# Normalized-query/key attention on one core: moving the Q and K transposes from TensorE to the DMA engines

## The chip, the cores and the metric

One core of one Trainium2 chip. The metric is device microseconds (us) of one execution. Executions of one kernel agree within about 0.3%. Engines in the profile: PE = TensorE matmuls, PEld = TensorE weight loads, DVE = VectorE, ACT = ScalarE, POOL = GpSimd, SP = SyncE (SPq is its queue of issued DMAs).

## The reference

```python
# q, k, v: (1, 32, 2048, 20) bf16; t: (32,) bf16
qn = q / (jnp.sqrt((q * q).sum(axis=-1, keepdims=True)) + eps)
kn = k / (jnp.sqrt((k * k).sum(axis=-1, keepdims=True)) + eps)
logits = jnp.einsum('bhqd,bhkd->bhqk', qn, kn) * t[None, :, None, None]
attn = softmax(logits)
return jnp.einsum('bhqk,bhkd->bhqd', attn, v)
```

There are 32 heads of 2048 rows, and a row has only 20 elements.

## The kernel before

Work is laid out as 32 heads x 2 passes (halves of the queries) x 16 rounds, 1024 rounds in all. In a round TensorE makes a 128 x 1024 block of scores S in PSUM (two matmuls), ScalarE takes its exponential into SBUF, and two rounds later TensorE multiplies it by V and accumulates (two PV matmuls). There are two S buffers.

```python
def plan_exp(self, n):
    Sps = self.Sps[n % 2]                 # 2 score buffers in PSUM
    Pb = self.Pbuf[n % self.NB]
    ... e.activation(Pb[:], Sps[:], AF.Exp), [(E, self.eS[n])] ...
def plan_S(self, n, h, p, kg, qq):
    ...                                   # cut
    if n >= 2:
        waits.append((A, self.a_exp[n - 2]))   # buffer is free again
```

Each head's q and k arrive with rows on partitions. VectorE normalizes them, TensorE transposes them in batches of 8 small matmuls (128 x 20 each) into PSUM, and VectorE copies the batch to SBUF. A head has four such batches, put at rounds 9 and 13 of the two passes of the head before. The output is transposed back in the same way, in two batches of 4 at rounds 2 and 6 of each pass.

```python
def plan_qt_transposes(self, h, bb):      # kt: the same with kn
    for i in range(n):                    # n = 8
        out_ap = self.TQK[0:self.D, P * i:P * (i + 1)]
        in_ap = qnb[:, tt, :]
        fn = lambda e, o=out_ap, a=in_ap: e.transpose(o, a, self.ident_bf[:, :])
        ...                               # cut
def plan_qt_copies(self, h, bb):
    dst = QTb[0:self.D, self.QH * bb:self.QH * (bb + 1)]
    ... e.tensor_copy(out=dst, in_=self.TQK[0:self.D, :]) ...
# in the loop over rounds
            if bg_idx < len(bgtasks):     # squared sums of heads 4 to 31 on VectorE
                self.ss_task(hh, qk)      # one task a round until done
```

Of the kernel before, what the change touches and what calls it, by code (L numbers as in the profile page):

```python
# [9 lines left out]
P = 128  # L10
# [19 lines left out]
class _Builder:  # L30
# [90 lines left out]
    def alloc(self):  # L121
# [7 lines left out]
        self.sDO = [self.sem("sDO0"), self.sem("sDO1")]  # L129
        groups = []  # L130
        hs = 0
        for he in (self.HA, min(self.H, 12), self.H):
            if he > hs:
                groups.append((hs, he))
                hs = he
# [22 lines left out]
        self.qn = [self.sb("qn%d" % b, [P, T, D], bf) for b in range(2)]  # L158
        self.kn = [self.sb("kn%d" % b, [P, T, D], bf) for b in range(2)]
# [8 lines left out]
        self.TQK = self.ps("TQK", [32, QH], bf)  # L168
# [3 lines left out]
    def plan(self):  # L172
# [11 lines left out]
        for gi, (hs, he) in enumerate(self.groups):  # L184
            for tens, store, sems in ((q, self.q_all, self.dq), (k, self.k_all, self.dk), (v, self.v_all, self.dv)):
                src = tens[0, hs:he].rearrange("h (p t) d -> p h (t d)", p=P)
                dst = store[:, hs:he, :, :].rearrange("p h t d -> p h (t d)")
                sy(lambda e, d=dst, s=src: e.dma_start(d, s), (), sems[gi], 16)

# [5 lines left out]
        self.g_qt = {}  # L195
        self.g_kt = {}
        for b in range(2):
            vb, qtb, ktb = self.vaug[b], self.QT[b], self.KT[b]
            self.g_qt[b] = gp(lambda e, qtb=qtb: e.memset(qtb[:], 0.0))  # L199
            self.g_kt[b] = gp(lambda e, ktb=ktb: e.memset(ktb[:], 0.0))  # L200
            gp(lambda e, vb=vb: e.memset(vb[:], 0.0))  # L201
            self.g_vaug[b] = gp(lambda e, vb=vb: e.memset(vb[:, :, D:D + 1], 1.0))
# [24 lines left out]
        self.v_qtcp_done = {}  # L227
        self.v_ktcp_done = {}
        self.tr_qt = {}
        self.tr_kt = {}  # L230
# [4 lines left out]
        self.last_tqkread_v = 0  # L235
# [6 lines left out]
        self.plan_qt_transposes(0, 0)  # L242
        self.plan_qt_copies(0, 0)
        self.plan_kt_transposes(0, 0)
        self.plan_kt_copies(0, 0)
# [12 lines left out]
        for n in range(NT):  # L258
# [13 lines left out]
            if h == 0 and p == 0:  # L272
                if r == 0:
                    self.plan_kt_transposes(0, 1)
                elif r == 3:
                    self.plan_qt_transposes(0, 1)
            if p == 0:
                if h >= 1:
                    if r == 2:
                        self.plan_O_transposes(h - 1, 1, 0)  # L280
                        self.plan_O_transposes(h - 1, 1, 1)
                    elif r == 6:
                        self.plan_O_transposes(h - 1, 1, 2)
                        self.plan_O_transposes(h - 1, 1, 3)
                if h + 1 < H:
                    if r == 9:
                        self.plan_qt_transposes(h + 1, 0)
                    elif r == 13:
                        self.plan_qt_transposes(h + 1, 1)
            else:  # L290
                if r == 2:
                    self.plan_O_transposes(h, 0, 0)
                    self.plan_O_transposes(h, 0, 1)
                elif r == 6:
                    self.plan_O_transposes(h, 0, 2)
                    self.plan_O_transposes(h, 0, 3)
                if h + 1 < H:
                    if r == 9:
                        self.plan_kt_transposes(h + 1, 0)
                    elif r == 13:  # L300
                        self.plan_kt_transposes(h + 1, 1)
            if h == 0 and p == 0:
                if r == 1:
                    self.plan_kt_copies(0, 1)
                elif r == 4:
                    self.plan_qt_copies(0, 1)
            if p == 0:
                if r == 0 and h >= 1:
                    self.plan_copyout(h - 1, 1, 0)
                if r == 1 and h >= 1:  # L310
                    self.plan_copyout(h - 1, 1, 1)
                if r == 2 and h + 1 < H:
                    self.plan_prep(h + 1)
                if r == 7 and h >= 1:
                    self.plan_divides(h - 1, 1)
                if h + 1 < H:
                    if r == 10:
                        self.plan_qt_copies(h + 1, 0)
                    elif r == 14:
                        self.plan_qt_copies(h + 1, 1)  # L320
            else:
                if r == 0:
                    self.plan_copyout(h, 0, 0)
                elif r == 1:
                    self.plan_copyout(h, 0, 1)
                elif r == 7:
                    self.plan_divides(h, 0)
                if h + 1 < H:
                    if r == 10:
                        self.plan_kt_copies(h + 1, 0)  # L330
                    elif r == 14:
                        self.plan_kt_copies(h + 1, 1)
            if bg_idx < len(bgtasks):
# [67 lines left out]
    def plan_prep(self, h):  # L401
# [3 lines left out]
        vaug, qnb, knb = self.vaug[b], self.qn[b], self.kn[b]  # L405
# [11 lines left out]
        w = [(self.dq[gi], 16)]  # L417
        if h >= 2:
            w.append((TR, self.tr_qt[(h - 2, 1)]))
        v2 = self.op("vector", lambda e: e.tensor_tensor(out=qnb[:], in0=qsrc,  # L420
# [6 lines left out]
        if h >= 2:  # L427
            w.append((TR, self.tr_kt[(h - 2, 1)]))
        v3 = self.op("vector", lambda e: e.tensor_tensor(out=knb[:], in0=ksrc,  # L429
# [3 lines left out]

    def plan_qt_transposes(self, h, bb):
        V, TR, G = self.sV, self.sTR, self.sG
        b = h % 2
        qnb = self.qn[b]
        n = self.QH // P
        waits0 = [(V, max(self.v_qn[h], self.last_tqkread_v)), (G, self.g_ident)]
        val = None  # L440
        for i in range(n):
            tt = bb * n + i
            out_ap = self.TQK[0:self.D, P * i:P * (i + 1)]
            in_ap = qnb[:, tt, :]
            fn = lambda e, o=out_ap, a=in_ap: e.transpose(o, a, self.ident_bf[:, :])  # L445
            val = self.op("tensor", fn, waits0 if i == 0 else (),
                          inc=(TR if i == n - 1 else None), chain=False)
        self.tr_qt[(h, bb)] = val
        return val

    def plan_kt_transposes(self, h, bb):
        V, TR, G = self.sV, self.sTR, self.sG
        b = h % 2
        knb = self.kn[b]
        n = self.QH // P
        waits0 = [(V, max(self.v_kn[h], self.last_tqkread_v)), (G, self.g_ident)]
        val = None
        for i in range(n):
            tt = bb * n + i
            out_ap = self.TQK[0:self.D, P * i:P * (i + 1)]  # L460
            in_ap = knb[:, tt, :]
            fn = lambda e, o=out_ap, a=in_ap: e.transpose(o, a, self.ident_bf[:, :])  # L462
            val = self.op("tensor", fn, waits0 if i == 0 else (),
                          inc=(TR if i == n - 1 else None), chain=False)
        self.tr_kt[(h, bb)] = val
        return val

    def plan_qt_copies(self, h, bb):
        V, TR, E, G = self.sV, self.sTR, self.sE, self.sG
        b = h % 2  # L470
        QTb = self.QT[b]
        waits = [(TR, self.tr_qt[(h, bb)])]
        if h >= 2:
            waits.append((E, self.ePV[self.end_round_of_head(h - 2)]))
        val = None
        waits.append((G, self.g_qt[b]))
        dst = QTb[0:self.D, self.QH * bb:self.QH * (bb + 1)]
        src = self.TQK[0:self.D, :]
        val = self.op("vector", lambda e: e.tensor_copy(out=dst, in_=src), waits, inc=V)  # L479
        self.last_tqkread_v = val  # L480
        self.v_qtcp_done[(h, bb)] = val
        return val

    def plan_kt_copies(self, h, bb):
        V, TR, E, G = self.sV, self.sTR, self.sE, self.sG
        b = h % 2
        KTb = self.KT[b]
        waits = [(TR, self.tr_kt[(h, bb)]), (G, self.g_kt[b])]
        if h >= 2:
            waits.append((E, self.ePV[self.end_round_of_head(h - 2)]))  # L490
        src = self.TQK[0:self.D, :]
        dst = KTb[0:self.D, self.QH * bb:self.QH * (bb + 1)]
        val = self.op("vector", lambda e: e.tensor_copy(out=dst, in_=src), waits, inc=V)  # L493
        self.last_tqkread_v = val
        self.v_ktcp_done[(h, bb)] = val
        return val

    def plan_S(self, n, h, p, kg, qq):
# [4 lines left out]
        kb = 0 if kg < self.KG // 2 else 1  # L503
        qb = min(p, 1)
        waits = [(V, max(self.v_ktcp_done[(h, kb)], self.v_qtcp_done[(h, qb)]))]
# [150 lines left out]
```

## Time and profile before

| | before |
|---|---|
| median of the runs, us | 1077.85 (1077.7 to 1078.46) |
| ScalarE busy, us | 973.5 (90%) |
| TensorE matmul busy, us | 1047.9 (97%) |
| VectorE busy, us | 308.1 (29%) |
| time of one pass in the steady stretch, us | 16.22 |

The page's groups of instructions of the kernel before. A line is: source line, engine, operation, out<-in, shapes, count | busy us, mean ns of one | idle us just before them and what ended it.

```profile
L550 ACT ACTIVATE Pbf<-Sps 128x1024 bf16<-128x1024 f32 x1024 | 966.0, 1031 | 89.7 <-PE Sps L516 89.7
L516 PE MATMUL Sps<-QT,KT 128*128 128x512 bf16 x2048 | 618.6, 384 | 5.2 <-ACT Pbf L550 4.4
...
L479 DVE COPY QT<-TQK 20x1024 bf16<-20x1024 bf16 x64 | 43.4, 679 | 179.4 <-PE TQK L445 178.9
```

The exponentials are busy for 966 us, and ScalarE stands idle for 90 us more, waiting for S.

Two lines of the chain of waits of the kernel before, shares of the span by engine and by line:

```profile
PE 91%; DVE 5%; ACT 1%; POOL 1%; issue 0%; ACTq 0%; DVEq 0%; POOLq 0%
PE Sps L516 42%; PE OACC L541 39%; PE TOps L589 4%; PE TQK L462 3%; PE TQK L445 3%; DVE ss_all L370 2%; DVE sq_tmp L367 1%; ACT Pbf L550 1%; DVE O_sb L569 0%; DVE QT L479 0%; POOL vaug L201 0%; POOL KT L200 0%; POOL QT L199 0%; DVE KT L493 0%; DVE qn L420 0%
```

The chain runs along TensorE, and 6% of the span is q and k transposes. ScalarE's timeline in the steady stretch shows where they hurt. Columns: start us, length us, engine, line, operation, count merged, and in brackets the idle time before and what ended it.

```profile
283.04 3.77 ACT L550 ACTIVATE Pbf<-Sps 128x1024 bf16<-128x1024 f32 x4 [0.18 <-PE Sps L516]
287.00 2.85 ACT L550 ACTIVATE Pbf<-Sps 128x1024 bf16<-128x1024 f32 x3 [0.19 <-PE Sps L516]
290.25 3.77 ACT L550 ACTIVATE Pbf<-Sps 128x1024 bf16<-128x1024 f32 x4 [0.39 <-PE Sps L516]
294.40 4.69 ACT L550 ACTIVATE Pbf<-Sps 128x1024 bf16<-128x1024 f32 x5 [0.38 <-PE Sps L516]
299.27 3.77 ACT L550 ACTIVATE Pbf<-Sps 128x1024 bf16<-128x1024 f32 x4 [0.18 <-PE Sps L516]
```

A pass is 16.23 us (283.04 to 299.27) and has four breaks. The two with 0.38 and 0.39 us idle follow the q/k transposes, the two with 0.18 and 0.19 us the output transposes.

### The profile page before, as it was taken

How to read it: one execution, taken by the hardware profiler on the slowest of the kernel's cores; microseconds unless marked ns; L12 is line 12 of the kernel's file. 1: busy time of each engine (PE TensorE's matmuls, PEld its weight loads, DVE VectorE, ACT ScalarE, POOL GpSimd, SP SyncE). 2: the span in 40 equal slices, each digit the busy share in tenths (PEclk: the TensorE clock that was granted, in tenths of full speed). 3: DMA queues.
4: the chain of work that ended last, by engine and by line, in shares of the span. 5: the costliest groups of instructions: out<-in, count | busy, mean ns of one | idle time of the engine just before them, and what ended most of it. 6: DMA issues, size and time to landing. Idle time of an engine off the chain costs nothing.

```text
span 1077.9 us, 13377 instructions
## 1 busy us (share of the span) xinstructions
PE 1047.9 (97%) x5632; PEld 438.2 (41%) x5632; DVE 308.1 (29%) x631; ACT 973.5 (90%) x1032; POOL 12.2 (1%) x16
## 2 busy tenths in 40 slices
PE   4989899999999999999999999999999999999998
PEld 1334344444444444444444444444444444444443
DVE  6993122222122222122222122222122222122221
ACT  3878899999999999999999999999999999999998
POOL 4000000000000000000000000000000000000000
PEclk9999899999999999999999999999999999999999
DMA  9000000000000000000000000000000000000000
GB/s 277 16 4 4 1 4 4 5 4 1 4 4 4 4 4 1 4 4 4 4 4 1 4 4 4 4 4 1 4 4 4 4 4 1 4 4 4 4 4 4
DMA packets 17244, 11.35 MB, mean 11 GB/s; under 512 B 800, under 2 KB 17184, under 8 KB 17184
## 3 DMA queue, kind: packets, MB, share of 16 engines
q1 hardware_dynamic: 17184, 10.50, 3.5%
q8 instruction: 44, 0.72, 0.3%
q14 instruction: 16, 0.13, 0.0%
HBM read 7.87 MB, written 2.62 MB: 10 GB/s over the span
## 4 chain that ended last, share of the span: by engine, by line
PE 91%; DVE 5%; ACT 1%; POOL 1%; issue 0%; ACTq 0%; DVEq 0%; POOLq 0%
PE Sps L516 42%; PE OACC L541 39%; PE TOps L589 4%; PE TQK L462 3%; PE TQK L445 3%; DVE ss_all L370 2%; DVE sq_tmp L367 1%; ACT Pbf L550 1%; DVE O_sb L569 0%; DVE QT L479 0%; POOL vaug L201 0%; POOL KT L200 0%; POOL QT L199 0%; DVE KT L493 0%; DVE qn L420 0%
## 5 line engine op out<-in xcount | busy, mean ns | idle before, releaser
L550 ACT ACTIVATE Pbf<-Sps 128x1024 bf16<-128x1024 f32 x1024 | 966.0, 1031 | 89.7 <-PE Sps L516 89.7
L516 PE MATMUL Sps<-QT,KT 128*128 128x512 bf16 x2048 | 618.6, 384 | 5.2 <-ACT Pbf L550 4.4
L541 PE MATMUL OACC<-Pbf,vaug 128*128 128x512 bf16 x2048 | 611.8, 381 | 3.2 <-DVE O_sb L569 2.9
L541 PEld LDWEIGHTS OACC<-Pbf,vaug 128*128 128x128 bf16 x2048 | 200.7, 98 | 248.6 <-DVE O_sb L569 4.3
L516 PEld LDWEIGHTS Sps<-QT,KT 128*128 128x128 bf16 x2048 | 139.5, 98 | 260.8 <-ACT Pbf L550 180.1
L569 DVE COPY O_sb<-OACC 21x512 f32<-21x512 f32 x128 | 86.9, 679 | 150.4 <-PE OACC L541 149.8
L493 DVE COPY KT<-TQK 20x1024 bf16<-20x1024 bf16 x64 | 43.5, 679 | 183.3 <-PE TQK L462 183.1
L479 DVE COPY QT<-TQK 20x1024 bf16<-20x1024 bf16 x64 | 43.4, 679 | 179.4 <-PE TQK L445 178.9
L605 DVE RECIPROCAL recip<-TOps 128x8 f32<-128x8 f32 x64 | 13.3, 208 | 235.9 <-PE TOps L589 235.7
L589 PEld LDWEIGHTS TOps<-ident_f,O_sb 21*128 21x128 f32 x512 | 41.2, 137 | 58.5 <-DVE O_sb L569 31.0
L589 PE MATMUL TOps<-ident_f,O_sb 21*128 21x21 f32 x512 | 54.1, 219 | 4.0 <-DVE O_sb L569 4.0
L445 PE MATMUL TQK<-ident_bf,qn 128*20 128x128 bf16 x512 | 39.8, 221 | 14.2 <-DVE qn L420 14.2
L445 PEld LDWEIGHTS TQK<-ident_bf,qn 128*20 128x20 bf16 x512 | 28.2, 92 | 40.9 <-issue 24.6
L462 PE MATMUL TQK<-ident_bf,kn 128*20 128x128 bf16 x512 | 40.2, 222 | 0.8 <-DVE QT L479 0.8
L462 PEld LDWEIGHTS TQK<-ident_bf,kn 128*20 128x20 bf16 x512 | 28.5, 92 | 28.2 <-issue 26.7
L370 DVE TENSOR_REDUCE ss_all<-sq_tmp 128x16 f32<-128x320 bf16 x56 | 27.2, 486 | 1.9
L610 DVE TENSOR_TENSOR out_st<-TOps,recip 128x160 bf16<-128x160 f32 x64 | 20.8, 325 | 4.3
L420 DVE TENSOR_TENSOR qn<-q_all,rsq_t 128x320 bf16<-128x320 bf16 x32 | 15.7, 491 | 1.1
L429 DVE TENSOR_TENSOR kn<-k_all,rs_all 128x320 bf16<-128x320 bf16 x32 | 15.7, 491 | 1.1
L367 DVE TENSOR_TENSOR sq_tmp<-q_all 128x320 bf16<-128x320 bf16 x28 | 9.1, 325 | 1.1
L367 DVE TENSOR_TENSOR sq_tmp<-k_all 128x320 bf16<-128x320 bf16 x28 | 9.1, 325 | 1.1
L218 ACT ACTIVATE ln_all<-ss_all 128x128 f32<-128x128 f32 x1 | 0.3, 310 | 9.1 <-DVE ss_all L211 9.1
(27 smaller groups left out, 43.2 us busy)
## 6 DMA issues: line engine op xcount, KB each, us to landing
out_dram<-out_st SPq DMA_DIRECT2D x32, 80.0 KB, 1.6
q_all<-in_q_dram SPq DMA_DIRECT2D x1, 1600.0 KB, 11.7
k_all<-in_k_dram SPq DMA_DIRECT2D x1, 1600.0 KB, 14.9
v_all<-in_v_dram SPq DMA_DIRECT2D x1, 1600.0 KB, 14.8
q_all<-in_q_dram SPq DMA_DIRECT2D x1, 640.0 KB, 7.4
k_all<-in_k_dram SPq DMA_DIRECT2D x1, 640.0 KB, 9.0
v_all<-in_v_dram SPq DMA_DIRECT2D x1, 640.0 KB, 9.4
q_all<-in_q_dram SPq DMA_DIRECT2D x1, 320.0 KB, 3.9
```

The costliest lines, as they stand in the source:

```text
L367: self.op("vector", lambda e: e.tensor_tensor(out=sq, in0=src, in1=src, op=ALU.mult), [(dsem, 16)], inc=V)
L370: return self.op("vector", lambda e: e.tensor_reduce(out=dst, in_=sq, axis=AX.X, op=ALU.add), [], inc=V)
L445: fn = lambda e, o=out_ap, a=in_ap: e.transpose(o, a, self.ident_bf[:, :])
L462: fn = lambda e, o=out_ap, a=in_ap: e.transpose(o, a, self.ident_bf[:, :])
L479: val = self.op("vector", lambda e: e.tensor_copy(out=dst, in_=src), waits, inc=V)
L493: val = self.op("vector", lambda e: e.tensor_copy(out=dst, in_=src), waits, inc=V)
L516: fn = lambda e, o=outap, l=lhsT, r=rhs: e.matmul(o, l, r, start=True, stop=True)
L541: fn = lambda e, o=outap, l=lhsT, rr=rhs, st=start, sp=stop: e.matmul(o, l, rr, start=st, stop=sp)
L550: val = self.op("scalar", lambda e: e.activation(Pb[:], Sps[:], AF.Exp), [(E, self.eS[n])], inc=self.sA)
L569: val = self.op("vector", lambda e: e.tensor_copy(out=Os[0:D1, c0:c1], in_=OA[0:D1, c0:c1]), waits, inc=V)
L589: fn = lambda e, o=out_ap, a=in_ap: e.transpose(o, a, self.ident_f[0:D1, 0:D1])
L610: v2 = self.op("vector", lambda e: e.tensor_tensor(out=dst, in0=TO[:, :, 0:D], in1=rec[:].to_broadcast([P, n, D]), op=ALU.mult), w2, inc=V)
```

## The change

The intent is to take the q/k transposes off TensorE and their copies off VectorE. Q and K are normalized into zero-padded 128-column tiles; a DMA transpose turns each whole tensor of a head (128 x 16 x 128 bf16, 512 KB). Two side measures: the last and largest group of loads (4.8 MB) is issued after the first head's transposes, and the squared-sum work skips every third round after round 16.

```diff
+        load(0)
+        load(1)
...
         self.plan_prep(0)
-        self.plan_qt_transposes(0, 0)
-        self.plan_qt_copies(0, 0)
-        self.plan_kt_transposes(0, 0)
-        self.plan_kt_copies(0, 0)
+        load(2)
...
-                if h + 1 < H:
-                    if r == 9:
-                        self.plan_qt_transposes(h + 1, 0)
...                                          (all transposes and copies of q and k removed)
-            if bg_idx < len(bgtasks):
+            if bg_idx < len(bgtasks) and (n < 16 or n % 3 != 2):
...
+        qout = QTb[:].rearrange("d (t p) -> d t p", p=P)
+        self.dqt_val[h] = self.op("sync", lambda e: e.dma_start_transpose(qout, qnTb[:]),
+                                  [(V, v2)] + sw, inc=self.sDQT[b], inc_by=16)
+        kout = KTb[:].rearrange("d (t p) -> d t p", p=P)
+        self.dkt_val[h] = self.op("sync", lambda e: e.dma_start_transpose(kout, knTb[:]),
+                                  [(V, v3)] + sw, inc=self.sDKT[b], inc_by=16)
...
-        waits = [(V, max(self.v_ktcp_done[(h, kb)], self.v_qtcp_done[(h, qb)]))]
+        waits = [(self.sDQT[b], self.dqt_val[h]), (self.sDKT[b], self.dkt_val[h])]
```

More of the change, by code (lines that the diff above doesn't have):

```diff
@@ L129, in alloc @@
         self.sDO = [self.sem("sDO0"), self.sem("sDO1")]
+        self.sDQT = [self.sem("sDQT0"), self.sem("sDQT1")]
+        self.sDKT = [self.sem("sDKT0"), self.sem("sDKT1")]
         groups = []
@@ L157, in alloc @@
         self.rsq_t = self.sb("rsq_t", [P, T], f32)
-        self.qn = [self.sb("qn%d" % b, [P, T, D], bf) for b in range(2)]
-        self.kn = [self.sb("kn%d" % b, [P, T, D], bf) for b in range(2)]
+        self.qnT = [self.sb("qnT%d" % b, [P, T, P], bf) for b in range(2)]
+        self.knT = [self.sb("knT%d" % b, [P, T, P], bf) for b in range(2)]
         self.vaug = [self.sb("vaug%d" % b, [P, T, P], bf) for b in range(2)]
@@ L167, in alloc @@
         self.Sps = [self.ps("Sps%d" % b, [P, QH], f32) for b in range(2)]
-        self.TQK = self.ps("TQK", [32, QH], bf)
         self.TO = self.ps("TOps", [P, QH // P, D + 1], f32)
@@ L183, in plan, with load @@
         self.v_dT = sy(lambda e: e.dma_start(tb[:], t.partition_broadcast(P)), (), self.sDT, 16)
-        for gi, (hs, he) in enumerate(self.groups):
+        def load(gi):
+            hs, he = self.groups[gi]
             for tens, store, sems in ((q, self.q_all, self.dq), (k, self.k_all, self.dk), (v, self.v_all, self.dv)):
@@ L194, in plan @@
         self.g_vaug = {}
-        self.g_qt = {}
-        self.g_kt = {}
+        self.g_qkt = {}
         for b in range(2):
-            vb, qtb, ktb = self.vaug[b], self.QT[b], self.KT[b]
-            self.g_qt[b] = gp(lambda e, qtb=qtb: e.memset(qtb[:], 0.0))
-            self.g_kt[b] = gp(lambda e, ktb=ktb: e.memset(ktb[:], 0.0))
+            vb, qtb, ktb = self.vaug[b], self.qnT[b], self.knT[b]
+            gp(lambda e, qtb=qtb: e.memset(qtb[:], 0.0))
+            self.g_qkt[b] = gp(lambda e, ktb=ktb: e.memset(ktb[:], 0.0))
             gp(lambda e, vb=vb: e.memset(vb[:], 0.0))
@@ L226, in plan @@
         self.v_vaug = {}
-        self.v_qtcp_done = {}
-        self.v_ktcp_done = {}
-        self.tr_qt = {}
-        self.tr_kt = {}
+        self.dqt_val = {}
+        self.dkt_val = {}
         self.tr_O = {}
@@ L234, in plan @@
         self.last_divmul_v = 0
-        self.last_tqkread_v = 0
         self.eS = {}
@@ L271, in plan @@
             self.plan_exp(n)
-            if h == 0 and p == 0:
-                if r == 0:
-                    self.plan_kt_transposes(0, 1)
-                elif r == 3:
-                    self.plan_qt_transposes(0, 1)
             if p == 0:
@@ L284, in plan @@
                         self.plan_O_transposes(h - 1, 1, 3)
-                if h + 1 < H:
-                    if r == 9:
-                        self.plan_qt_transposes(h + 1, 0)
-                    elif r == 13:
-                        self.plan_qt_transposes(h + 1, 1)
             else:
@@ L296, in plan @@
                     self.plan_O_transposes(h, 0, 3)
-                if h + 1 < H:
-                    if r == 9:
-                        self.plan_kt_transposes(h + 1, 0)
-                    elif r == 13:
-                        self.plan_kt_transposes(h + 1, 1)
-            if h == 0 and p == 0:
-                if r == 1:
-                    self.plan_kt_copies(0, 1)
-                elif r == 4:
-                    self.plan_qt_copies(0, 1)
             if p == 0:
@@ L315, in plan @@
                     self.plan_divides(h - 1, 1)
-                if h + 1 < H:
-                    if r == 10:
-                        self.plan_qt_copies(h + 1, 0)
-                    elif r == 14:
-                        self.plan_qt_copies(h + 1, 1)
             else:
@@ L327, in plan @@
                     self.plan_divides(h, 0)
-                if h + 1 < H:
-                    if r == 10:
-                        self.plan_kt_copies(h + 1, 0)
-                    elif r == 14:
-                        self.plan_kt_copies(h + 1, 1)
-            if bg_idx < len(bgtasks):
+            if bg_idx < len(bgtasks) and (n < 16 or n % 3 != 2):
                 hh, qk = bgtasks[bg_idx]
@@ L404, in plan_prep @@
         T, D = self.T, self.D
-        vaug, qnb, knb = self.vaug[b], self.qn[b], self.kn[b]
+        vaug, qnTb, knTb = self.vaug[b], self.qnT[b], self.knT[b]
         gi = self.grp_of_head[h]
@@ L416, in plan_prep @@
         qsrc = self.q_all[:, h]
-        w = [(self.dq[gi], 16)]
+        w = [(self.dq[gi], 16), (G, self.g_qkt[b])]
         if h >= 2:
-            w.append((TR, self.tr_qt[(h - 2, 1)]))
-        v2 = self.op("vector", lambda e: e.tensor_tensor(out=qnb[:], in0=qsrc,
+            w.append((self.sDQT[b], self.dqt_val[h - 2]))
+        qdst = qnTb[:, :, 0:D]
+        v2 = self.op("vector", lambda e: e.tensor_tensor(out=qdst, in0=qsrc,
                                                          in1=rst[:].unsqueeze(2).to_broadcast([P, T, D]),
@@ L427, in plan_prep @@
         if h >= 2:
-            w.append((TR, self.tr_kt[(h - 2, 1)]))
-        v3 = self.op("vector", lambda e: e.tensor_tensor(out=knb[:], in0=ksrc,
+            w.append((self.sDKT[b], self.dkt_val[h - 2]))
+        kdst = knTb[:, :, 0:D]
+        v3 = self.op("vector", lambda e: e.tensor_tensor(out=kdst, in0=ksrc,
                                                          in1=rsk.unsqueeze(2).to_broadcast([P, T, D]),
@@ L432, in plan_prep @@
         self.v_kn[h] = v3
-    def plan_qt_transposes(self, h, bb):
-        V, TR, G = self.sV, self.sTR, self.sG
-        b = h % 2
-        qnb = self.qn[b]
-        n = self.QH // P
-        waits0 = [(V, max(self.v_qn[h], self.last_tqkread_v)), (G, self.g_ident)]
-        val = None
-        for i in range(n):
-            tt = bb * n + i
-            out_ap = self.TQK[0:self.D, P * i:P * (i + 1)]
-            in_ap = qnb[:, tt, :]
-            fn = lambda e, o=out_ap, a=in_ap: e.transpose(o, a, self.ident_bf[:, :])
-            val = self.op("tensor", fn, waits0 if i == 0 else (),
-                          inc=(TR if i == n - 1 else None), chain=False)
-        self.tr_qt[(h, bb)] = val
-        return val
@@ L451, in plan_kt_transposes @@
-    def plan_kt_transposes(self, h, bb):
-        V, TR, G = self.sV, self.sTR, self.sG
-        b = h % 2
-        knb = self.kn[b]
-        n = self.QH // P
-        waits0 = [(V, max(self.v_kn[h], self.last_tqkread_v)), (G, self.g_ident)]
-        val = None
-        for i in range(n):
-            tt = bb * n + i
-            out_ap = self.TQK[0:self.D, P * i:P * (i + 1)]
-            in_ap = knb[:, tt, :]
-            fn = lambda e, o=out_ap, a=in_ap: e.transpose(o, a, self.ident_bf[:, :])
-            val = self.op("tensor", fn, waits0 if i == 0 else (),
-                          inc=(TR if i == n - 1 else None), chain=False)
-        self.tr_kt[(h, bb)] = val
-        return val
@@ L468, in plan_qt_copies @@
-    def plan_qt_copies(self, h, bb):
-        V, TR, E, G = self.sV, self.sTR, self.sE, self.sG
-        b = h % 2
-        QTb = self.QT[b]
-        waits = [(TR, self.tr_qt[(h, bb)])]
-        if h >= 2:
-            waits.append((E, self.ePV[self.end_round_of_head(h - 2)]))
-        val = None
-        waits.append((G, self.g_qt[b]))
-        dst = QTb[0:self.D, self.QH * bb:self.QH * (bb + 1)]
-        src = self.TQK[0:self.D, :]
-        val = self.op("vector", lambda e: e.tensor_copy(out=dst, in_=src), waits, inc=V)
-        self.last_tqkread_v = val
-        self.v_qtcp_done[(h, bb)] = val
-        return val
@@ L484, in plan_kt_copies @@
-    def plan_kt_copies(self, h, bb):
-        V, TR, E, G = self.sV, self.sTR, self.sE, self.sG
-        b = h % 2
-        KTb = self.KT[b]
-        waits = [(TR, self.tr_kt[(h, bb)]), (G, self.g_kt[b])]
-        if h >= 2:
-            waits.append((E, self.ePV[self.end_round_of_head(h - 2)]))
-        src = self.TQK[0:self.D, :]
-        dst = KTb[0:self.D, self.QH * bb:self.QH * (bb + 1)]
-        val = self.op("vector", lambda e: e.tensor_copy(out=dst, in_=src), waits, inc=V)
-        self.last_tqkread_v = val
-        self.v_ktcp_done[(h, bb)] = val
-        return val
+        QTb, KTb = self.QT[b], self.KT[b]
@@ new lines, in plan_prep @@
+        sw = []
+        if h >= 2:
+            sw.append((E, self.ePV[self.end_round_of_head(h - 2)]))
+        qout = QTb[:].rearrange("d (t p) -> d t p", p=P)
[4 more added lines that the diff above has]
+                                  [(V, v3)] + sw, inc=self.sDKT[b], inc_by=16)
@@ L502, in plan_S @@
         Sps = self.Sps[n % 2]
-        kb = 0 if kg < self.KG // 2 else 1
-        qb = min(p, 1)
-        waits = [(V, max(self.v_ktcp_done[(h, kb)], self.v_qtcp_done[(h, qb)]))]
+        waits = [(self.sDQT[b], self.dqt_val[h]), (self.sDKT[b], self.dkt_val[h])]
         if n >= 2:
```

## The prediction

> **What bounds the kernel now.** It does 1024 rounds (32 heads x 2 passes x 16), each one exponential on ScalarE, two S and two PV matmuls. The timeline shows exponentials back to back at 0.943 us; 1024 are 966 us (groups table). A round's four matmuls take 0.86 us in the chain of waits. So ScalarE is the floor and TensorE only 0.08 us per round behind; every extra batch on TensorE breaks ScalarE's run. ScalarE's timeline at 270 to 335 us repeats every 16.22 us (one pass) with four gaps: 0.19, 0.39, 0.38, 0.18 us. The two large ones follow the q/k transposes (8 small matmuls, 0.55 us in the chain), the small ones the output transposes. The chain is 91% TensorE, 6% q/k transposes.
>
> **What the change does.** It removes 1024 TensorE transposes and 128 VectorE copies (679 ns each, mostly not critical). It adds 64 DMA transposes on the SP queue, each 128 x 16 x 128 bf16 = 512 KB (20 columns padded to 128). The third group of loads moves behind the first head's transposes; squared-sum work is thinned after round 16.
>
> **Gain.** Per head the q/k gaps are 4 x 0.385 = 1.54 us; over 31 heads 48 us. The output gaps (4 x 0.185 per head) stay. Between 20 and 134 us ScalarE idles about 19 us, against 8 at the steady share: VectorE is 90% busy until 80 us and the granted clock drops to 0.73 in places. Fewer copies and thinner sums may give back 4 us; head 0's own extra transposes 1 us.
>
> **Loss.** q and k are normalized at 14.2 and 14.7 us and the first S starts at 17.8. Now two DMA transposes in one queue lie between: first S at 22 to 24 us, 5 us lost.
>
> **Is the DMA hidden?** A head's pair is issued about two rounds into the head before and must land within about 28 us. The Trainium skill, "DMA: Bandwidth & Descriptors", section "Latency and other measured facts", gives 261 GB/s for one measured DMA transpose: 2.0 us for 512 KB. This trace's loads moved 640-byte rows at up to 311 GB/s, 2.06 ns a row; 2048 rows of 256 bytes at that row rate take 4.2 us (estimate). With the 1.6 us an 80 KB store takes to land: 4 to 6 us each, 8 to 12 a pair, hidden. The other reading: "VectorE: DVE Perf Modes", section "The three transpose paths", gives 1309 ns for a 128x128 DMA transpose. I take that as mostly fixed cost; paid serially for 16 blocks, one would be 21 us, a pair 42 us per head against a period of 31, and the kernel DMA-bound at about 1360 us. No run yet tells which.
>
> **Predicted time.** 1078 - 48 - 5 + 5 = 1030 us; range 1020 to 1062. Chances: faster by over 2% 0.75, within 2% 0.05, slower 0.20.
>
> **What would show it.** Right: ScalarE's gaps per pass fall from four to two of about 0.19 us; pass period 15.4 to 15.5 us; TensorE waits for the transposes only at the first head, perhaps a little at the second (its pair queues behind 4.8 MB of loads); they land in 4 to 6 us. Wrong: S matmuls waiting at every head's start, landing times over about 14 us each; or the output gaps growing into those removed; or a lower granted clock.
>
> **What would make it wrong.** A per-block or per-row cost of the DMA transpose several times my estimate; transposes blocking instruction fetch or stores on the same DMA engines; the second head starved by the late loads.

## The result, and the profile after

The changed kernel takes 1012.33 us (median of 8 runs, 1011.62 to 1014.05) against 1077.75 us for the kernel before (15 runs, those of these rounds included). The ratio is 0.9394, 95% interval 0.9385 to 0.9403. Ratios here are the mean time of one kernel's fast runs over that of the other's of the same rounds, so not quite the ratio of the medians. The sign was right, but the time lies below the predicted range of 1020 to 1062 us.

The groups of the changed kernel that answer to those above:

```profile
L463 ACT ACTIVATE Pbf<-Sps 128x1024 bf16<-128x1024 f32 x1024 | 952.6, 1057 | 36.3 <-PE Sps L429 36.3
L429 PE MATMUL Sps<-QT,KT 128*128 128x512 bf16 x2048 | 619.0, 384 | 24.8 <-DMA KT<-knT 20.1
```

Its DMA issues: out<-in, queue, operation, count, median us from issue to landing (no size is given for transposes):

```profile
QT<-qnT SPq DMA_TRANSPOSE x32, 3.9
KT<-knT SPq DMA_TRANSPOSE x32, 4.1
```

Two things are to be seen. TensorE's matmuls waited for a DMA transpose in one place only, the 20.1 us before the first S; every other transpose was hidden. And the exponentials' own busy time fell by 13.4 us (966.0 to 952.6), although not one of them was changed, while the mean length of one rose from 1031 to 1057 ns.

The chain of waits of the changed kernel:

```profile
PE 95%; ACT 2%; POOL 1%; DVE 1%; DMA 0%; issue 0%; ACTq 0%; DVEq 0%; POOLq 0%
PE Sps L429 47%; PE OACC L454 43%; PE TOps L502 4%; ACT Pbf L463 2%; DVE O_sb L482 0%; DMA KT<-knT 0%; POOL vaug L204 0%; POOL knT L203 0%; POOL qnT L202 0%; DVE ss_all L337 0%; DVE sq_tmp L334 0%; ACT L361 0%; ACT L360 0%; ACT rs_all L361 0%; ACT ln_all L360 0%
```

The TQK lines are gone; the chain still follows TensorE. ScalarE's timeline in the steady stretch of the changed kernel:

```profile
277.77 3.77 ACT L463 ACTIVATE Pbf<-Sps 128x1024 bf16<-128x1024 f32 x4 [0.18 <-PE Sps L429]
281.73 11.10 ACT L463 ACTIVATE Pbf<-Sps 128x1024 bf16<-128x1024 f32 x12 [0.18 <-PE Sps L429]
293.01 3.77 ACT L463 ACTIVATE Pbf<-Sps 128x1024 bf16<-128x1024 f32 x4 [0.18 <-PE Sps L429]
296.97 11.10 ACT L463 ACTIVATE Pbf<-Sps 128x1024 bf16<-128x1024 f32 x12 [0.18 <-PE Sps L429]
```

A pass is 15.24 us (281.73 to 296.97), with the two output breaks as predicted, but shorter than the predicted 15.4 to 15.5. The lengths say why. A run of 4 lasts 3.77 us and a run of 12 lasts 11.10 us, so 8 more exponentials cost 7.33 us, 0.916 each. A run of n is then 1.02 + 0.916 (n - 1): the first of a run costs about 0.11 us more, because it overlaps with nothing. The Trainium skill, "ScalarE: Activation LUTs", section "What ACT_TABLE_LOAD costs", describes such an overlap: back-to-back activations overlap by about 93 ns. Here it is about 108 ns (1.024 us for the first of a run, 0.916 for each further one). So a break costs its idle gap and 0.11 us more, and the second part is booked as busy time.

Where the 66.8 us between the two profiled runs (1077.9 and 1011.1) come from, with the starts of the passes worked out from ScalarE's timelines:

| stretch | before | after | difference | predicted |
|---|---|---|---|---|
| start to first exponential | 18.9 | 21.2 | +2.3 | +5 |
| passes 1 to 6 | 115.1 | 101.1 | -14.0 | about -9.6 |
| passes 7 to 62, 56 x (16.22 - 15.24) | | | -55 | -43 |
| last two passes and the end | | | about 0 | 0 |

The predicted column splits the prediction's 48 us over 62 passes (0.77 each) and adds its 5 us to the first six.

### The profile page after: what moved, and what is told of

It reads as the page before. It is cut to its first block, busy times and chain, and to the rows that moved or that the text cites. A ratio compares the mean times of both kernels' runs of the same rounds, so it can differ in the third digit from the quotient of the medians.

```text
span 1011.1 us, 11259 instructions
## 1 busy us (share of the span) xinstructions
PE 980.7 (97%) x4608; PEld 370.4 (37%) x4608; DVE 221.5 (22%) x503; ACT 960.1 (95%) x1032; POOL 12.2 (1%) x16
## 4 chain that ended last, share of the span: by engine, by line
PE 95%; ACT 2%; POOL 1%; DVE 1%; DMA 0%; issue 0%; ACTq 0%; DVEq 0%; POOLq 0%
PE Sps L429 47%; PE OACC L454 43%; PE TOps L502 4%; ACT Pbf L463 2%; DVE O_sb L482 0%; DMA KT<-knT 0%; POOL vaug L204 0%; POOL knT L203 0%; POOL qnT L202 0%; DVE ss_all L337 0%; DVE sq_tmp L334 0%; ACT L361 0%; ACT L360 0%; ACT rs_all L361 0%; ACT ln_all L360 0%
## 5 line engine op out<-in xcount | busy, mean ns | idle before, releaser
L463 ACT ACTIVATE Pbf<-Sps 128x1024 bf16<-128x1024 f32 x1024 | 952.6, 1057 | 36.3 <-PE Sps L429 36.3
L429 PE MATMUL Sps<-QT,KT 128*128 128x512 bf16 x2048 | 619.0, 384 | 24.8 <-DMA KT<-knT 20.1
L429 PEld LDWEIGHTS Sps<-QT,KT 128*128 128x128 bf16 x2048 | 129.2, 97 | 336.3 <-ACT Pbf L463 266.6
L388 DVE TENSOR_TENSOR qnT<-q_all,rsq_t 128x320 bf16<-128x320 bf16 x32 | 15.8, 493 | 3.6 <-DVE rsq_t L381 0.5
L398 DVE TENSOR_TENSOR knT<-k_all,rs_all 128x320 bf16<-128x320 bf16 x32 | 15.8, 492 | 3.5 <-DVE qnT L388 0.5
L378 DVE COPY vaug<-v_all 128x320 bf16<-128x320 bf16 x32 | 7.8, 245 | 1.9 <-DVE O_sb L482 0.5
L381 DVE TENSOR_SCALAR rsq_t<-rs_all,t_f 128x16 f32<-128x16 f32 x32 | 7.5, 234 | 1.1
L202 POOL MEMSET qnT<- 128x2048 bf16 x2 | 3.6, 1805 | 0.1
L203 POOL MEMSET knT<- 128x2048 bf16 x2 | 3.6, 1805 | 0.1
L204 POOL MEMSET vaug<- 128x2048 bf16 x2 | 3.6, 1805 | 0.1
L350 DVE TENSOR_REDUCE ss_all<-sq_tmp 128x64 f32<-128x1280 bf16 x2 | 3.0, 1486 | 0.1
```

The costliest lines, as they stand in the source:

```text
L378: vv = self.op("vector", lambda e: e.tensor_copy(out=vaug[:, :, 0:D], in_=vsrc), waits, inc=V)
L388: v2 = self.op("vector", lambda e: e.tensor_tensor(out=qdst, in0=qsrc, in1=rst[:].unsqueeze(2).to_broadcast([P, T, D]), op=ALU.mult), w, i ...
L398: v3 = self.op("vector", lambda e: e.tensor_tensor(out=kdst, in0=ksrc, in1=rsk.unsqueeze(2).to_broadcast([P, T, D]), op=ALU.mult), w, inc=V)
L429: fn = lambda e, o=outap, l=lhsT, r=rhs: e.matmul(o, l, r, start=True, stop=True)
L463: val = self.op("scalar", lambda e: e.activation(Pb[:], Sps[:], AF.Exp), [(E, self.eS[n])], inc=self.sA)
```

## The experiments

Theory A: each batch of small matmuls breaks ScalarE's run, and the cost is the gap plus the lost overlap. Theory B: only the gap counts, and the further 14 us came from the copies taken off VectorE, or from one of the side measures. All twelve kernels gave correct results.

### pe8: the batches back on TensorE, unused

```diff
+    def plan_dummy(self, cnt):
+        for i in range(cnt):
+            o = self.TQK[0:self.D, P * i:P * (i + 1)]
+            ... e.transpose(o, self.ident_bf[:, 0:self.D], self.ident_bf[:, :]) ...
...
+            if h + 1 < H and r in (9, 13):
+                self.plan_dummy(8)
```

> The changed kernel with the q/k transposes put back on TensorE as dummies (8 small matmuls at the same four places per head, result unused, no copies on VectorE); the DMA transposes still do the work. Theory A (each batch breaks ScalarE's run: a gap of 0.385 us and 0.11 us more because the first exponential after a gap is not overlapped with the one before it): 124 breaks x 0.495 = 61 us, so 1073 us, and a steady pass back at 16.2 us. Theory B (only the gap counts, and the other 14 us of the gain came from the copies taken off VectorE): 48 us, so 1060 us and a pass of 16.0 us.

Measured: 1073.24 us (4 runs, 1072.98 to 1073.89), ratio to before 0.9955. The steady pass is back at 16.22 us. That is 60.9 us over the changed kernel, or 0.49 us for each of the 124 batches: theory A's number, not the 48 us of the gaps alone. ScalarE's timeline of this run, one pass (300.87 to 317.09), has the four breaks of the kernel before:

```profile
300.87 3.77 ACT L472 ACTIVATE Pbf<-Sps 128x1024 bf16<-128x1024 f32 x4 [0.38 <-PE Sps L438]
305.02 4.69 ACT L472 ACTIVATE Pbf<-Sps 128x1024 bf16<-128x1024 f32 x5 [0.38 <-PE Sps L438]
309.90 3.77 ACT L472 ACTIVATE Pbf<-Sps 128x1024 bf16<-128x1024 f32 x4 [0.18 <-PE Sps L438]
313.85 2.86 ACT L472 ACTIVATE Pbf<-Sps 128x1024 bf16<-128x1024 f32 x3 [0.18 <-PE Sps L438]
317.09 3.77 ACT L472 ACTIVATE Pbf<-Sps 128x1024 bf16<-128x1024 f32 x4 [0.38 <-PE Sps L438]
```

The copies are still absent, so they have no part in it.

### copies: the VectorE copies back, unused

```diff
+            if h + 1 < H and r in (10, 14):
+                self.op("vector", lambda e: e.tensor_copy(out=self.cp_scr[0:D, :], in_=self.TQK[0:D, :]), ...)
```

> The changed kernel with the 128 VectorE copies put back (124 of them, PSUM to SBUF, 20x1024, result unused), no extra TensorE work. Theory A: ScalarE never waits for VectorE in the steady stretch, so a pass stays at 15.24 us and the time at 1012 to 1016 us (a little in the busy start). Theory B (copies slow the exponentials or delay TensorE): 14 us more, 1026 us, pass 15.46 us.

Measured: 1011.99 us (4 runs, 1011.4 to 1013.21), steady pass 15.24 us. The 124 copies, 84 us of VectorE time, cost nothing. (To have something to copy, this run also makes one batch of eight small matmuls at the start.) Theory B falls with these two runs.

### pe2 and pe4: smaller batches

The same edit with 2 and 4 in place of 8.

> The changed kernel with dummy batches of 2 small matmuls instead of 8, same places. Theory A with slack: gaps of 0.385 us for a 0.55 us batch and 0.185 for a 0.36 us batch extrapolate to no gap at about 0.18 us, and 2 matmuls are about 0.14 us, so no break and 1012 to 1017 us. Rival (cost proportional to TensorE work, TensorE being the bound): a quarter of 61 us, 1027 us.

Measured: 1032.09 us (4 runs, 1031.56 to 1032.88). The expectation failed: small batches do not hide. It cost even more than the proportional rival said. ScalarE's timeline of this run:

```profile
484.34 3.77 ACT L472 ACTIVATE Pbf<-Sps 128x1024 bf16<-128x1024 f32 x4 [0.18 <-PE Sps L438]
488.30 11.41 ACT L472 ACTIVATE Pbf<-Sps 128x1024 bf16<-128x1024 f32 x12 [0.18 <-PE Sps L438]
499.90 3.77 ACT L472 ACTIVATE Pbf<-Sps 128x1024 bf16<-128x1024 f32 x4 [0.18 <-PE Sps L438]
```

No break is shown where the dummy batches are: the 12 exponentials still stand as one run. But it lasts 11.41 us instead of 11.10, 0.155 us more for each of its two batches. The timeline merges instructions whose idle time between them is under 0.15 us, and names no wait for it; the total of the group has it:

```profile
L472 ACT ACTIVATE Pbf<-Sps 128x1024 bf16<-128x1024 f32 x1024 | 965.6, 1030 | 41.9 <-PE Sps L438 35.9
```

Of 41.9 us of idle time 35.9 are named. The other 6.0 are 0.048 us for each of the 124 batches, and 0.048 + 0.108 is 0.156. So theory A's sum, the gap and the lost overlap, holds here too. What failed was my extrapolation from the gaps to a batch that costs nothing: the overlap is lost before a gap opens.

> The changed kernel with dummy batches of 4 small matmuls (0.27 us). Theory A with slack: a gap of about 0.1 us plus the restart of 0.11 us, 124 x 0.21 = 26 us, 1038 us; the trace shows breaks at all four places with gaps of 0.05 to 0.15 us. Proportional rival: half of 61 us, 1043 us. Gap-only rival without a restart cost: 12 us, 1024 us.

Measured: 1045.18 us (4 runs, 1044.83 to 1046.9). The pass is 15.78 us, 0.27 us per batch, with recorded gaps of 0.16 and 0.15 us; 0.155 + 0.108 is 0.26. So a break does cost the gap and the lost overlap, which the gap-only rival (1024 us) denies. But the gap was larger than I had put it with the slack in mind (0.1 us), and the time 7 us above theory A's 1038, close to the proportional rival.

### pe1: a test of the line through the others

> The changed kernel with dummy batches of one small matmul. The runs with 2, 4 and 8 lie on 0.043 us + 0.056 us per matmul, so 0.10 us a batch, 124 x 0.10 = 12 us, 1024 us, with no idle gap recorded on ScalarE at those places: the loss shows only as runs of exponentials that last longer. If a batch of one hides wholly: 1012 us.

Measured: 1024.74 us (4 runs, 1024.43 to 1025.27), as expected. ScalarE's timeline of this run:

```profile
485.14 11.30 ACT L472 ACTIVATE Pbf<-Sps 128x1024 bf16<-128x1024 f32 x12 [0.19 <-PE Sps L438]
496.62 3.77 ACT L472 ACTIVATE Pbf<-Sps 128x1024 bf16<-128x1024 f32 x4 [0.18 <-PE Sps L438]
```

One small matmul, no gap (the two exponentials still overlap, by about 0.01 us), and the run of 12 is 0.20 us longer for two of them.

| matmuls in a batch | steady pass, us | cost of a batch, (pass - 15.24) / 2 | idle time of ScalarE at a batch, us | S to S across a batch, us |
|---|---|---|---|---|
| 1 | 15.44 | 0.10 | none | 1.12 |
| 2 | 15.55 | 0.155 | 0.05 | 1.17 |
| 4 | 15.78 | 0.27 | 0.155 | 1.29 |
| 8 | 16.22 | 0.49 | 0.38 | 1.51 |

The last column is the time on TensorE from the first matmul of one S block to that of the next with a batch between them (medians of the traces from 200 to 900 us).

The cost is 0.043 us and 0.056 us per matmul, from the first one on. 0.056 us is also the start-to-start time that the Trainium skill gives for a matmul of 128 columns ("TensorE: Matmul & The Clock Gate", section "Wait — 56ns, not 53.3ns?"): each further small matmul delays ScalarE by its own length. Why one matmul of 0.056 us already costs 0.10 is seen on TensorE in the run pe1 (its PV matmuls, which lie between these lines, are left out):

```profile
484.50 0.61 PE L438 MATMUL Sps<-QT,KT 128*128 128x512 bf16 x2
485.37 0.60 PE L438 MATMUL Sps<-QT,KT 128*128 128x512 bf16 x2
486.23 0.59 PE L438 MATMUL Sps<-QT,KT 128*128 128x512 bf16 x2
...
487.19 0.22 PE L419 MATMUL TQK<-ident_bf 128*20 128x128 bf16 x1
487.35 0.60 PE L438 MATMUL Sps<-QT,KT 128*128 128x512 bf16 x2
```

In the rounds after a break S follows S in 0.86 or 0.87 us, faster than ScalarE's 0.916, so TensorE does have a lead there. Across the batch of one it is 1.12 us. The batch thus takes about 0.26 us of TensorE, 0.20 more than its matmul; with 2, 4 and 8 matmuls the excess is 0.20 again (1.17, 1.29 and 1.51 less 0.86 and less 0.056 for each matmul). About 0.16 us of each batch is absorbed before ScalarE, and 0.043 + 0.056 per matmul is what is left. The lead does shelter something, but the fixed part of a batch alone is more than it can shelter. What the fixed 0.20 us consists of no run separates.

### ospread: the output transposes in smaller batches

```diff
-                    if r == 2:
-                        self.plan_O_transposes(h - 1, 1, 0)
-                        self.plan_O_transposes(h - 1, 1, 1)
...
+                    if r in (2, 5, 8, 11):
+                        self.plan_O_transposes(h - 1, 1, (r - 2) // 3)
...
-                if r == 7 and h >= 1:
+                if r == 12 and h >= 1:
```

> The changed kernel with the output transposes in four batches of 2 per pass instead of two of 4. Slack theory (small batches hide): 0.3 us less per batch, up to 38 us faster, 975 us. After the dose runs (a fixed part of about 0.04 us per batch and a cost proportional to its matmuls, no slack): four batches of about 0.19 us against two of 0.30 us, 0.16 us more per pass, so about 10 us slower, 1022 us.

Measured: 1019.2 us (4 runs, 1019.0 to 1020.49), 6.9 us slower than the changed kernel. (The divisions of the output move from round 7 to round 12 to follow the last batch.) ScalarE's timeline shows no break, in this line 36 exponentials, but the group's total again has idle time too short to be named, 16.6 of 29.3 us, about 0.07 us a batch:

```profile
469.31 34.65 ACT L455 ACTIVATE Pbf<-Sps 128x1024 bf16<-128x1024 f32 x36
```

```profile
L455 ACT ACTIVATE Pbf<-Sps 128x1024 bf16<-128x1024 f32 x1024 | 965.7, 1034 | 29.3 <-PE Sps L421 12.7
```

36 undisturbed ones would take 1.02 + 35 x 0.916 = 33.1 us. ScalarE is busy for 687.85 of the 700 us between 200 and 900 us (98.3%), in the changed kernel for 683.25 (97.6%): the slower kernel has the busier ScalarE.

### odma: the output transposes on the DMA as well

```diff
-        self.O_sb = self.sb("O_sb", [32, QH], f32)
+        self.O_sb = self.sb("O_sb", [32, QH], bf)
+        self.OT = self.sb("OT", [P, QH // P, 32], bf)
...
+        self.tr_O[(h, p)] = self.op("sync", lambda e: e.dma_start_transpose(OT[:], Os[:]), ...)
...
-        TO, rec = self.TO, self.rec
+        TO, rec = self.OT, self.rec
```

> The changed kernel with the output transposes taken off TensorE as well: the copies out of the accumulator write bf16, a DMA transpose of 32 x 1024 turns them, the division reads SBUF. No break is left in ScalarE's run: a pass is 16 exponentials at 0.916 us = 14.65 us, 0.59 less than 15.24, so 64 x 0.59 = 38 us less: 975 us, ScalarE busy over 97% outside the start. Rival (TensorE then bounds, or the DMA's latency delays the accumulator's reuse): 985 us or more, S or PV matmuls waiting.

Measured: 975.84 us (4 runs, 975.42 to 977.11), correct, ratio to before 0.906. This version beats both kernels. With no batch left on TensorE the run does not break, and the spacing is that of full overlap:

```profile
469.25 34.06 ACT L452 ACTIVATE Pbf<-Sps 128x1024 bf16<-128x1024 f32 x37
```

```profile
L452 ACT ACTIVATE Pbf<-Sps 128x1024 bf16<-128x1024 f32 x1024 | 939.7, 1118 | 10.9 <-PE Sps L418 10.5
```

The pass is 14.67 us, 0.57 less than 15.24, two breaks of 0.29. (The output passes through bf16 before the division here, a rounding that the changed kernel does not have.) The busy time of the same 1024 exponentials fell by another 13 us, and the mean of one rose to 1118 ns, since an overlapped one is recorded from before its predecessor ends.

### order, nothin, before_thin: the side measures

order moves the third group of loads back in front of the first transposes.

> The changed kernel with the old order of loads: the third group (4.8 MB) is issued before the first head's two DMA transposes. Theory: the transposes queue behind it, the first S starts at about 33 to 37 us instead of 20.1, and the whole is 12 to 16 us longer, 1024 to 1028 us, nothing else changed. Rival (DMA engines serve the transposes at once beside the loads): 1012 to 1014 us.

Measured: 1026.79 us (4 runs, 1024.94 to 1027.28), first exponential at 34.5 us instead of 21.2, steady pass 15.24 us. As expected. Issues of SP in this run, start us and length us:

```profile
14.46 5.52 SPq L190 DMA_DIRECT2D v_all<-in_v_dram  x1
20.03 9.16 SPq L407 DMA_TRANSPOSE QT<-qnT  x1
29.24 1.73 SPq L410 DMA_TRANSPOSE KT<-knT  x1
```

The first transpose is issued at 20.0 us instead of 14.2 and is held for 9 us behind the loads. The order of issue in the change is worth 14 us.

nothin takes the thinning out of the changed kernel (`if bg_idx < len(bgtasks):`); before_thin puts the thinning alone into the kernel before.

> The changed kernel without the thinning of the squared-sum work (a task in every round until they are done). If the thinning is what gave back 8 us more than the steady share in the first six passes, this run is 5 to 8 us slower (1018 to 1020 us) with passes 1 to 3 near 17.5 us. If it was the absence of the copies and the transposes, it is within 3 us of 1012.

Measured: 1015.84 us (4 runs, 1015.58 to 1015.98), 3.5 us slower: between the two alternatives. The pass lengths were 15.7, 16.0, 16.8, 18.1, 19.8, 17.5 us, against 16.0, 16.0, 15.2, 15.9, 20.5, 17.5 with thinning.

> The kernel before with only the thinning of the squared-sum work. If thinning alone relieves VectorE in the first passes: 4 to 8 us faster than before, 1070 to 1074 us. If VectorE's copies of QT and KT were what crowded it: within 2 us of before.

Measured: 1072.58 us (4 runs, 1072.54 to 1074.67), 5.0 us faster, as the first alternative said. What a crowded VectorE does is seen in the kernel before, at the fourth pass:

```profile
75.41 0.68 DVE L569 COPY O_sb<-OACC 21x512 f32<-21x512 f32 x1
76.15 0.60 PE L541 MATMUL OACC<-Pbf,vaug 128*128 128x512 bf16 x2 [1.95 <-DVE O_sb L569]
77.07 0.68 DVE L569 COPY O_sb<-OACC 21x512 f32<-21x512 f32 x1
77.81 0.61 PE L589 MATMUL TOps<-ident_f,O_sb 21*128 21x21 f32 x4 [1.05 <-DVE O_sb L569]
78.35 1.04 PE L516 MATMUL Sps<-QT,KT 128*128 128x512 bf16 x2
79.18 1.06 PE L541 MATMUL OACC<-Pbf,vaug 128*128 128x512 bf16 x2
79.43 1.02 ACT L550 ACTIVATE Pbf<-Sps 128x1024 bf16<-128x1024 f32 x1 [4.05 <-PE Sps L516]
```

The copy out of the accumulator comes late, TensorE stands for 1.95 and 1.05 us, and for the next 5 us its pairs of matmuls take 1.04 to 1.06 us instead of 0.60; the granted clock in the stretch from 79 to 84 us was 0.51. ScalarE lost 4.05 us there. The Trainium skill describes such a fall to half clock after idling ("TensorE: Matmul & The Clock Gate", section "What's actually happening"), and this trace agrees in so far as 0.51 follows these waits; no run changes the idling alone.

### dma4 and dma8: how much the DMA could bear

```diff
+        for i in range(6):                # dma8: 14
+            self.op("sync", lambda e, o=scr, s=(qnTb if i % 2 == 0 else knTb): e.dma_start_transpose(o, s[:]), ...)
         self.dqt_val[h] = self.op("sync", lambda e: e.dma_start_transpose(qout, qnTb[:]),
```

The copies go to scratch, and the next use of the normalized tiles waits for them.

> The changed kernel with three extra copies of each DMA transpose into scratch, 8 per head instead of 2, queued ahead of the two that matter. From the trace a pair occupies the queue about 4 us and lands in 5.9 us, so about 2.0 to 2.5 us each, 16 to 20 us per head, still inside the 28 us window: steady pass unchanged at 15.24 us; the start gets 12 to 15 us longer because the extras stand ahead of the first pair: about 1026 us. Rival (a transpose costs 128x128 blocks serially, or the engines disturb ScalarE and TensorE): passes longer.

Measured: 1028.66 us (4 runs, 1026.98 to 1028.97), first exponential at 34.6 us, steady pass 15.24 us. Four times as many transposes are still hidden; only the start pays (S waited for transposes twice, at the first two heads).

> The same with 16 transposes per head. At 2.0 to 2.5 us each 32 to 40 us per head, over the 30.5 us of compute: S matmuls wait at every head's start for the transposes and the kernel is bound by them at 32 x 32 to 40 us, 1060 to 1310 us. The period per head over 16 is the throughput cost of one transpose.

Measured: 1392.36 us (4 runs, 1389.4 to 1398.33), more than the upper end that I gave. Issues of SP from one head to the next:

```profile
607.98 1.57 SPq L415 DMA_TRANSPOSE dscr<-qnT  x1
...
639.46 1.72 SPq L421 DMA_TRANSPOSE KT<-knT  x1
641.22 0.58 SPq L547 DMA_DIRECT2D out_dram<-out_st  x1
649.47 1.56 SPq L415 DMA_TRANSPOSE dscr<-qnT  x1
```

16 transposes are issued in 33.2 us (607.98 to 641.18), 2.1 us each, as expected. What I left out is that the queue then idles for 7.7 us: the next head's transposes wait for the last PV of the head before, and in program order that PV stands behind the first two S of the new head, which wait for the transposes that have just been issued. After that PV the queue still waits, about 2.4 us, for VectorE to normalize the next head's tiles. The period is 41.5 us.

## Why the prediction was right or wrong

- **Which breaks go: right.** The two breaks of 0.38 us per pass went, the two output breaks of 0.18 us stayed, and no wait for the DMA appeared after the start.
- **The DMA transposes: right.** They land in 3.9 and 4.1 us (predicted 4 to 6), and a pair lands in about 6 us since the second is issued while the first moves. The first reading of the prediction, 261 GB/s ("DMA: Bandwidth & Descriptors", section "Latency and other measured facts"), is borne out: 524,288 bytes in 2.1 us are 250 GB/s. The serial reading, 21 us each, is not. (The prediction's 2.0 us and 21 us for one transpose were estimates from the two pages' figures.)
- **The step that failed: "Per head the q/k gaps are 4 x 0.385 = 1.54 us; over 31 heads 48 us."** The term is mis-sized. Removing a break saves 0.49 us, not 0.385: the lost overlap of 0.11 us comes back too. With it goes the floor of "exponentials back to back at 0.943 us; 1024 are 966 us": 0.943 is a run of four, 3.77 / 4, with one restart in it. Undisturbed the spacing is 0.916 us, 938 us for 1024. Shown by pe8 (+60.9 us for 124 batches), by the pass of 14.67 us in odma, and by exclusion in copies. It accounts for 12 of the 18 us between prediction and result (-55 against -43 in passes 7 to 62).
- **The start: sign right, size off.** First S at 20.1 us, not 22 to 24, and the first exponential 2.3 us later instead of 5, because the two transposes overlap.
- **The busy first passes: underestimated.** 14.0 us gained against 9.6. The thinning gives 3.5 us in one kernel and 5.0 in the other. The copies alone are not it: with them back and the thinning in place (copies) the first six passes took 99.7 us against 101.1. The steady saving is 5.9 us of the 14.0 (six times 0.98). The largest single part lies in the fourth pass, 22.3 us before and 16.0 after: there the kernel before has the late copy and the half clock shown above, and the changed kernel runs at a granted clock of 1.00 from 74 to 84 us. With the thinning alone (before_thin) that pass takes 16.9 us. How the rest divides was not separated.
- **The slack: an unstated belief that fell.** Expecting pe2 to be free, I believed that short batches would vanish in TensorE's lead. They do not, and ospread, pe1 and pe2 show it: a batch takes TensorE about 0.20 us on top of its matmuls, and only about 0.16 us is absorbed. So one matmul costs ScalarE 0.10 us.

## What to carry to other kernels

When the bounding engine gains by overlapping its own successive instructions, count what each interruption costs from the lengths of runs (here 3.77 us for 4 and 11.10 us for 12), not from the idle gaps: part of the cost is booked as busy time, and a short interruption leaves a gap that the timeline does not show, or none. Count also what a batch takes of the engine that feeds it beyond its own instructions (here 0.20 us a batch): splitting such work into more and smaller batches then makes it dearer (ospread), so move it to an engine with no part in the loop. Before trusting a hidden DMA, find its throughput by multiplying it: here four times as many still hid, and eight times did not.

## What the Trainium skill lacked or had wrong

- "ScalarE: Activation LUTs", section "What ACT_TABLE_LOAD costs": it has the overlap of back-to-back activations, 93 ns; for exponentials of 1024 columns from PSUM the runs show about 108 ns (1.024 us for the first of a run, 0.916 us for each further one). The prediction had not used it.
- "Perfetto Trace Analysis", section "Identifying the Most-Contended Engine": it calls occupancy a fair measure of how close ScalarE is to roofline. Here ScalarE was 98.3% busy at 15.35 us a pass (ospread), 97.6% at 15.24 us (the changed kernel) and 97.6% at 15.44 us (pe1): lost overlap counts as busy, so the busier kernel is not the faster one.
- "VectorE: DVE Perf Modes", section "The three transpose paths": it gives 1309 ns for a 128x128 DMA transpose and does not say how that grows. Sixteen such blocks in one instruction land in 3.9 to 4.1 us and cost 2.1 us each instruction when queued back to back, 0.13 us a block. The figure of the DMA page, 261 GB/s, is the one that carried over.
